# A state-space scan with a routed expert layer on one core: recurrence moved to TensorE and ScalarE, packed score products, one mask operation, six experts loaded before routing ends, and new tables of order

## The chip, the cores and the metric

The kernel runs as one program on one core of a Trainium2 chip. The metric is the device time of that program in microseconds (us), the median of repeated runs. The profile beside it comes from one execution, recorded by the hardware profiler.

## The reference

A chunked state-space scan over `(4 batches, 8 heads, 768 steps, 32 values)` with a state of 16 by 32 per batch and head gives a matrix of 3072 tokens by 256. That matrix goes through a layer of 8 experts: each token goes to the expert with the largest logit, each expert keeps its 80 tokens with the largest gate weight, and all other rows of the output are zero.

```python
cum = np.cumsum(la, axis=-1)                       # la: log of the decay, one chunk
L = np.exp(cum[..., :, None] - cum[..., None, :]) * causal
y_intra = np.einsum('bhij,bhjd->bhid', np.einsum('bhin,bhjn->bhij', Cc, Bc) * L, xc)
y_inter = np.einsum('bhin,bhnd->bhid', Cc, state) * np.exp(cum)[..., None]
state = decay_full[:, :, None, None] * state + np.sum(Bx, axis=2)
...
expert_idx = np.argmax(logits, axis=1)
for e in range(E):
    if len(tok_idx) > capacity:
        tok_idx = tok_idx[np.argpartition(-gw, capacity)[:capacity]]
    h = np.maximum(x[tok_idx] @ w1[e], 0.0)
    out[tok_idx] = gate_w[tok_idx, None] * (h @ w2[e])
```

## The kernel before, in words

**Order of the work.** The scheduling is manual: every engine runs its instructions in the order in which the program's text issues them, and waits only for what an instruction needs. The scan is cut into 12 chunks of 64 steps. The main loop runs over k = 0 to 10; its pass k finishes chunk k and prepares chunk k+1, and k = 11 stands behind the loop by itself. Between the fixed steps the loop calls `slot(plan, i)`, which reads letters from the table `PLAN[k]`: `k` is one step of a routing key, `t` spreads finished keys, `S` and `D` are rank comparisons on ScalarE and VectorE, `s` and `d` shorter ones, `o` and `O` comparisons of a tile with itself on GpSimd and VectorE, `c` the column sums of a comparison on TensorE, `w` a filler product. `LAST` and `REST` order what is left after chunk 11. `WARM` counts filler products at fixed places.

**One chunk.** TensorE multiplies chunk k+1's B by a block-diagonal copy of C (`scores`, tile `cb`): `bd` holds 8 heads side by side with 16 live rows each, so each product contracts all 128 rows to 32 columns, 4 of them 512 wide and 4 half as wide. The first three chunks' blocks are made by 24 scalings on ScalarE and VectorE (`first_blocks`, L683 and L685), the later ones by 8 small transfers per pair of chunks on SP's queue (`spread`, L325), which wait for VectorE's `ct` (`scale_c`, L319). Then come the router's `logits` (tile `rk`), the chunk's sums B times x (`chunk_sums`, tile `vs`, two banks), the part of the output from the state (`inter`), and the part within the chunk (`intra`, tile `yv`). VectorE masks the scores in two operations (`masks`, L346) and adds the carried state to the sums in two (`add_sums`, L368). GpSimd scales x (`scale_x`, L295), writes the state into a block layout by four operations of 32 partitions (`states`, L378, tile `stw`) and the decayed state by one (L384). ScalarE raises the exponents (`widen`, L306), which TensorE turns (`turn`, L312), copies the output (`save_outputs`, L411) and, after TensorE has turned it to token order (`turn_outputs`, L425, tile `mi`), copies it again for the transfer to `y_dram` (`store`, L429).

**Routing.** `keys` (L445 to L509) makes one number per token from the logits, some 22 small VectorE operations per group of 1 or 2 chunks. `turn_keys` lays keys out along the free dimension, and 276 blocks of 128 by 128 comparisons (`take`, L584 and L590) count how many keys of the same expert are larger. `collect` turns ranks into row numbers.

**Experts.** Weights of 4 experts are loaded during the scan (`load_w1`, `load_w2`, L274 and L279, 1 MB each), those of the other 4 into the same buffers as these come free, from SP's queue, one expert's 2 MB per job. `up` and `down` are 64 recorded TensorE products each; rows come by indirect transfers of GpSimd (`gather`, L918) and leave by others (`put_rows`, L976). Filler rows of the output are zeroed by three 1 MB transfers (`clear`, L284).

Line 120 is a helper that issues nearly all products, so profile rows of L120 are told apart by their tiles.

Of the kernel before, what the change touches and what calls it, by code (L numbers as in the profile page):

```python
# [7 lines left out]
F32 = mybir.dt.float32  # L8
# [9 lines left out]
P = 128  # L18
# [13 lines left out]
YT_BUFS = 3  # L32
SP = 4
WARM = (6, 2, 2, 4, 2, 11, 0, 1)
# [3 lines left out]
B0 = (1, 4, 7), ()  # L38
B1 = (0, 1, 4, 7), ()
B2 = (0, 1, 2, 3, 4, 5, 6, 7), ()  # L40
KS = 6
PAIRS = ()
POOLK = ()
POOLS = 15
MOVE = 0
BACK = 1
FAST = 7
PLAN = (
    "||||||",
    "||||||",  # L50
    "||kkk|||kk|sk",
    "||||||",
    "OSSO|c|kkkcc||||",
    "kkkS|||Sc||d|c",
    "||kkkcc||kS|kk|kkk",
    "ckOkkSS||kkkkkkkkc|c||S|kkktk",
    "cOODS|S|kkDccDkkkkkc||S||kkOckk",
    "SSkoct|Ssk|kDkckkkcSk|c|||DS",
    "kStocDSSc|k|kkk|c||dh||",
    "StDckSkkkkkk|cocDcSo|ScS|tkkkhDSckDkkckkoS|Scc|czScc|ccSccccchDkzkcc",  # L60
)
LAST = "ODsiDxiiScSiwDSiicwwiiiwiScwiwSwiDSwciiixcccz"
# [4 lines left out]
C_ID = C_W + 2 * P  # L67
C_H8 = C_ID + P
C_TIE = C_H8 + NH
C_SEL = C_TIE + P  # L70
C_MASK = C_SEL + P
C_WE = C_MASK + 2 * CH
C_BM = C_WE + NE
C_HM = C_BM + 16
C_TH = C_HM + 2
# [9 lines left out]
def const_block():  # L85
# [28 lines left out]
def moe_kernel(ctx: ExitStack, tc: tile.TileContext, cap, tm_d, bn_d, cn_d, aa_d, wg_d, w1_d, w2_d,  # L114
# [15 lines left out]
    cmp_bufs = 5 if cap <= 80 else 3  # L130
# [925 lines left out]
```

## Time and profile before

| what | us |
|---|---|
| median of 3 runs (lowest, highest) | 180.26 (179.71, 183.33) |
| time of the profiled execution | 182.07 |
| its span, first to last instruction | 180.3 |
| start, to the scores of chunk 1 | 0 to 14.66 |
| main loop | 14.66 to 98.55 |
| chunk 11, last keys and comparisons | 98.55 to 117.3 |
| row numbers and first gathers | 117.3 to 125.6 |
| eight experts, last transfer | 125.6 to 180.3 |

In a row of the timeline stand start, duration, engine, line, operation, output and inputs, the number of instructions merged, and in brackets how long the engine had been idle and what ended that. A row of the groups ends with busy time and mean duration of one, then idle time ahead of it. "issue" is idle time for which the trace shows no releaser. A row of the stretches gives the length, then the busy time of PE (TensorE's products), PEld (its weight loads), DVE (VectorE), ACT (ScalarE) and POOL (GpSimd) with instruction counts, the granted TensorE clock, the share of time in which the transfer engines were busy, and what they moved in GB/s. Recorded product durations overlap, so their count times the mean is more than their busy time.

### The profile page before, as it was taken

To read this page: it belongs to the slowest core of one execution; us is meant where nothing else is said; L and a number is where in the kernel's file an instruction comes from. 1 tells how busy PE (TensorE), PEld (TensorE's weight loads), DVE (VectorE), ACT (ScalarE), POOL (GpSimd) and SP (SyncE) were. 2 spreads that over 40 slices of the span, in tenths; PEclk is the share of its full clock that TensorE was granted. 3 is DMA by queue.
4 is the path that set the end of the run, shared out by engine and by line. 5 is a ranking of instruction groups with operands and counts; after the bars stand their busy time and mean duration, and the time that the engine had idled before them with its cause. 6 is when DMAs were issued, how large, how long until landed. Compare 5 with 4: busy or idle time off the path is not lost. (4 is left out here: it accounts for less than half of the span.)

```text
span 180.3 us, 8266 instructions
## 1 busy us (share of the span) xinstructions
PE 144.9 (80%) x3574; PEld 109.2 (61%) x3574; DVE 106.1 (59%) x430; ACT 71.1 (39%) x177; POOL 89.2 (49%) x147
## 2 busy tenths in 40 slices
PE   6578898389859857995998957879988797799980
PEld 2334566276547637583857847734977677689970
DVE  6499549456993999699999999970211011011100
ACT  3795322114225061727677979800212211221120
POOL 8280699363755638149585888907140340422022
PEclk9979999958999997599669955557999999999998
DMA  5981649985993995899653101101399999810000
GB/s 135 344 319 27 215 149 268 317 296 153 343 401 93 293 358 199 230 295 379 219 170 130 62 4 62 58 2 40 105 369 306 291 374 307 297 35 4 22 22 18
DMA packets 22549, 34.75 MB, mean 193 GB/s; under 512 B 2032, under 2 KB 17136, under 8 KB 22512
## 3 DMA queue, kind: packets, MB, share of 16 engines
q1 hardware_dynamic: 21744, 32.91, 54.8%
q0 software_dynamic: 768, 1.31, 2.4%
q8 instruction: 28, 0.46, 1.0%
q14 instruction: 9, 0.07, 0.1%
HBM read 26.08 MB, written 6.95 MB: 183 GB/s over the span
## 5 line engine op out<-in xcount | busy, mean ns | idle before, releaser
L378 POOL TENSOR_TENSOR stw<-rr,alr 32x256 f32<-32x256 f32 x44 | 27.1, 616 | 34.8 <-DVE rr L368 17.4
L976 POOL DMA_INDIRECT out<-og,idx x8 | 7.5, 935 | 37.9 <-DVE og L974 37.9
L120 PE MATMUL yv<-ht,w 128*64 128x80 f32 x512 | 20.8, 235 | 5.6 <-ACT ht L947 5.6
L120 PEld LDWEIGHTS yv<-ht,w 128*64 128x64 f32 x512 | 18.6, 137 | 7.2 <-ACT ht L947 6.4
L120 PE MATMUL cb<-bd,bn 128*32 128x512 f32 (+1 forms) x192 | 20.5, 535 | 2.2 <-ACT ep L306 1.0
L120 PE MATMUL yv<-ct,stw 128*64 128x64 f32 x320 | 17.2, 252 | 6.1 <-issue 5.4
L120 PE MATMUL cb<-xs,w 128*64 128x80 f32 x512 | 20.9, 234 | 0.4 <-DVE xs L931 0.4
L346 DVE TENSOR_TENSOR m<-cb,cst 128x512 f32<-128x512 f32 x24 | 15.4, 684 | 9.2 <-PE cb L120 9.2
L584 ACT ACTIVATE bd<-krow,keb 128x896 bf16<-128x896 f32 (+3 forms) x21 | 20.7, 991 | 0.0
L947 ACT ACTIVATE ht<-cb 128x320 f32<-128x320 f32 x16 | 7.0, 438 | 34.0 <-issue 11.3
L120 PEld LDWEIGHTS cb<-xs,w 128*64 128x64 f32 x512 | 18.9, 137 | 2.0 <-issue 1.3
L120 PEld LDWEIGHTS yv<-ct,stw 128*64 128x64 f32 x320 | 13.5, 157 | 8.2 <-issue 6.4
L974 DVE TENSOR_SCALAR og<-vs,gs 80x256 f32<-80x256 f32 x8 | 3.8, 480 | 24.4 <-PE vs L969 24.4
L429 ACT COPY zs<-mi 128x512 f32<-128x512 f32 x11 | 6.4, 584 | 28.3 <-PE mi L425 27.0
L295 POOL TENSOR_TENSOR xt<-tm,em 128x256 f32<-128x256 f32 x24 | 14.8, 636 | 5.3 <-ACT ep L306 3.5
L931 DVE COPY xs<-mi 128x160 f32<-128x160 f32 x8 | 2.6, 325 | 23.3 <-remote 12.6
L120 PEld LDWEIGHTS cb<-bd,bn 128*32 128x32 f32 x192 | 6.0, 117 | 12.6 <-issue 10.7
L120 PE MATMUL yv<-m,xt 64*32 64x64 f32 x704 | 11.6, 241 | 0.0
L590 DVE TENSOR_SCALAR_CACHE_REDUCE bd<-krow,keb 128x896 bf16<-128x896 f32 (+4 forms) x11 | 11.1, 1018 | 0.3
L918 POOL DMA_INDIRECT xg<-y_dram,idx x8 | 7.9, 991 | 6.6 <-issue 6.6
L120 PE MATMUL vs<-xt,tm 64*32 64x64 f32 x352 | 6.2, 231 | 5.5 <-issue 5.5
L120 PEld LDWEIGHTS yv<-m,xt 64*32 64x32 f32 x704 | 7.7, 117 | 3.5 <-issue 2.7
(153 smaller groups left out, 285.6 us busy)
## 6 DMA issues: line engine op xcount, KB each, us to landing
w<-w SPq DMA_DIRECT2D x16, 1024.0 KB, 7.5
tm<-tm SPq DMA_DIRECT2D x5, 768.0 KB, 6.0
y_dram<-zs SPq DMA_DIRECT2D x12, 256.0 KB, 2.6
out<-zrow SPq DMA_DIRECT2D x3, 1024.0 KB
cn<-cn SPq DMA_DIRECT2D x6, 256.0 KB, 6.1
bn<-bn SPq DMA_DIRECT2D x6, 256.0 KB, 3.9
bd<-ct SPq DMA_DIRECT2D x32, 32.0 KB, 5.5
tm<-tm SPq DMA_DIRECT2D x2, 384.0 KB, 5.9
```

The lines of the kernel that those rows point to most:

```text
L120: T.matmul(out=o, lhsT=l, rhs=r, start=start, stop=stop, skip_group_check=True, **kw)
L295: G.tensor_tensor(out=xt[:, p].rearrange("p (h d) -> p h d", h=NH), in0=tm[:, p].rearrange("p (h d) -> p h d", h=NH), in1=em[:, p, c, :, N ...
L346: V.tensor_tensor(out=m, in0=cb[p].rearrange("p (h i) -> p h i", h=NH), in1=cst[:, None, C_MASK + p * CH:C_MASK + (p + 1) * CH].broadcast_ ...
L378: G.tensor_tensor(out=stw[(c + 1) % 2][q, hp].rearrange("p b (r d) -> p (b r) d", r=2), in0=rr[q].rearrange("p b (r d) -> p (b r) d", r=2) ...
L429: S.copy(out=zs.rearrange("p t d -> p (t d)"), in_=z)
L584: S.activation(out=cmpt[:, 0:n], in_=rows, func=AF.Sign, scale=2.0 ** -24 - 1.0, bias=keb[:, t:t + 1], accum_out=acs[:, t, col:col + 1])
L590: V.tensor_scalar(out=cmpt[:, 0:n], in0=rows, scalar1=keb[:, t:t + 1], scalar2=None, op0=ALU.is_le, op1=ALU.add, accum_out=acc[:, t, col:c ...
L918: G.indirect_dma_start(out=xg[n % NX][0:cw], out_offset=None, in_=y_dram[:, :], in_offset=bass.IndirectOffsetOnAxis(ap=idx[0:cw, s, e:e + ...
L931: V.tensor_copy(out=xs, in_=mi[:, 0:2 * P].rearrange("p (k t) -> p k t", k=2)[:, :, 0:cw])
L947: S.activation(out=ht[:, f - 3:f + 1], in_=cb[f // 4].rearrange("p (f t) -> p f t", f=4)[:, :, 0:cw], func=AF.Relu)
L974: V.tensor_scalar(out=og[0:cw], in0=vs[n % 2][0:cw, 0:D], scalar1=gs[0:cw, s, e:e + 1], scalar2=None, op0=ALU.mult)
L976: G.indirect_dma_start(out=out, out_offset=bass.IndirectOffsetOnAxis(ap=idx[0:cw, s, e:e + 1], axis=0), in_=og[0:cw], in_offset=None, boun ...
```

## The change

Heads and batches are laid out in another order, so that a pair of heads fills 32 partitions. `bd` then needs 2 blocks per chunk in place of 8, and is made from `ct` by one ScalarE and one VectorE operation for every chunk; `spread`, `first_blocks` and their transfers are gone. `scores` becomes 16 products of 32 rows by 64 columns, 128 wide. The exponents go through 8 products of 64 by 64. The state has no block layout: TensorE adds it to the chunk's sums by a product with the identity, ScalarE copies the sum, GpSimd scales it in one operation. The two masks become one operation of 1024. The logits become 8 further columns of the product that turns the output. `vs` is one bank, `cb`, `yv` and `mi` are pairs of banks. GpSimd memsets of `bd` and `stw` at the start are gone, the first clip of `a` is split in two, constants come in three transfers by order of use. Weights come in parts of 512 KB with rows laid out contiguously by the host: six experts before routing ends, the last two during jobs 1 to 4. Some loads wait for a one-element write ("token") of VectorE, ScalarE or GpSimd into their target. `out` is cleared in 12 pieces. `BACK` goes from 1 to 5, and the tables are new.

```diff
-WARM = (6, 2, 2, 4, 2, 11, 0, 1)
+WARM = (8, 3, 5, 4, 2, 8, 0, 2)
...
-    "kStocDSSc|k|kkk|c||dh||",
+    "SSSSt|c|Sllwskckwkz|hwDS|D|OokDSoOocO|Scckll|",
...
+    def load_ahead(n):
+        i = order.index(jobs[n][0])
+        if slow and order.index(slow[0][0]) < i + W_EARLY + W_LATE:
+            load_slow(hold)
...
+    def scale_c(c, u, act):
+        cts[c] = ct = work.tile([P, 256], F32, name="ct", bufs=5)
+        V.tensor_tensor(out=ct, in0=cns[c], in1=u, op=ALU.mult)
+        for r in range(2):
+            o, m = bd[c % 3][:, r], cst[:, C_HM + r:C_HM + r + 1]
+            if r < act:
+                S.activation(out=o, in_=ct, func=AF.Copy, scale=m)
+            else:
+                V.tensor_scalar(out=o, in0=ct, scalar1=m, scalar2=None, op0=ALU.mult)
...
+    def scores(c):
+        for b in range(NB):
+            for g in range(2):
+                for q in range(2):
+                    r = slice(g * CH + 32 * q, g * CH + 32 * q + 32)
+                    mm(cb[q][g * CH:(g + 1) * CH, b * P:(b + 1) * P].rearrange("p (r i) -> p r i", r=2),
+                       bn[r, b * CH:(b + 1) * CH], bdc[r, :, b * CH:(b + 1) * CH], b == 0, True,
+                       tile_position=(r.start, g * CH))
...
     def masks(c):
+        m = work.tile([P, 2 * NH, CH], F32, name="m")
+        V.tensor_tensor(out=m, in0=cb2.rearrange("p q (h i) -> p (q h) i", h=NH),
+                        in1=cst[:, None, C_MASK:C_MASK + CH].broadcast_to([P, 2 * NH, CH]), op=ALU.mult)
...
     def chunk_sums(c):
+        if c:
+
+            mm(vs[:, 0:256], ident, stw[c % 2], False, True)
...
     def add_sums(c):
+        rr = work.tile([P, 256], F32, name="rr")
+        S.copy(out=rr, in_=vs[:, 0:256])
...
     def states(c):
-        for hp in range(4):
-            q = slice(32 * hp, 32 * hp + 32)
-            G.tensor_tensor(out=stw[(c + 1) % 2][q, hp].rearrange("p b (r d) -> p (b r) d", r=2),
...
+        G.tensor_tensor(out=stw[(c + 1) % 2].rearrange("p (b d) -> p b d", d=HD),
...
     def turn_outputs(c, z):
+                mm(z[:, p, g * P:(g + 1) * P + NE], yts[c][:, p, g], wi[:, g], g == 0, True)
```

**TensorE in one chunk.** Before, chunk 2, from the end of its scores to the first half of the second state product (`vs` and `yv` are pairs of banks, told apart by their numbers; `rk<-wg,yt` are the logits, `vs<-cst,ep` the turned exponents):

```order
L120 MATMUL cb_82<-bd_118,bn 32x8x32
L120 MATMUL rk<-wg,yt 32x8 x16
L120 MATMUL vs_85<-xt,tm 32x64 x8
L120 MATMUL vs_86<-xt,tm 32x64 x8
L120 MATMUL yv_83<-ct,stw_119 64x64 x4
L120 MATMUL yv_84<-ct,stw_119 64x64 x4
L120 MATMUL yv_83<-m,xt 32x64 x8
L120 MATMUL yv_84<-m,xt 32x64 x8
L312 MATMUL vs_85<-cst,ep 128x128 x2
L312 MATMUL vs_86<-cst,ep 128x128 x2
L120 MATMUL yv_83<-ct,stw_119 64x64 x4
```

And a whole chunk of the change, chunk 1 (`vs<-stw,cst` is the state added by the identity, `mi<-wi,yt` the turned output with the logits, `rk<-zer,ones` a filler):

```order
L118 MATMUL cb<-bd_121,bc 64x128 x16
L118 MATMUL vs<-xt,tm 32x64 x16
L118 MATMUL vs<-stw_123,cst 128x256
L118 MATMUL mi<-wi,yt 128x136 x4
L118 MATMUL yv<-ct,stw_123 64x64 x16
L118 MATMUL yv<-m,xt 32x64 x16
L118 MATMUL vs<-cst,ep 64x64 x8
L118 LDWEIGHTS ones
L118 MATMUL rk<-zer,ones 128x192
L118 MATMUL yv<-m,xt 32x64 x16
```

The logits are gone as a step, the turned output has moved from behind the state products to ahead of them, the state products stand in one piece, and one product with the identity is new.

**GpSimd in two chunks.** Before, from x of chunk 3 on:

```order
L295 TENSOR_TENSOR xt<-tm,em 128x256 x2
L378 TENSOR_TENSOR stw_119<-rr,alr 32x256 x4
L384 TENSOR_TENSOR st<-rr,alp 128x256
L295 TENSOR_TENSOR xt<-tm,em 128x256 x2
L378 TENSOR_TENSOR stw_120<-rr,alr 32x256 x4
```

The same place in the change:

```order
L348 TENSOR_TENSOR xt<-tm,em 128x256 x2
L404 TENSOR_TENSOR stw_122<-rr,alr 128x256
L326 MEMSET tm 1x1
L326 MEMSET zrow 1x1
L348 TENSOR_TENSOR xt<-tm,em 128x256 x2
```

Five operations on the state became one, with two one-element tokens behind it.

**SP's queue around the experts.** Before, the last stores of the scan and the first loads of the experts stage:

```order
L430 DMA y_dram<-zs 128x2x256 x3
L274 DMA w_2683<-w 128x2x1024
L279 DMA w_2685<-w 128x8x256
L274 DMA w_2771<-w 128x2x1024
L279 DMA w_2773<-w 128x8x256
```

In the change (rows of 1024 values are the 512 KB parts):

```order
L311 DMA out<-zrow 256x1x256 x2
L303 DMA w_2233<-w 128x1024 x2
L303 DMA w_2323<-w 128x1024 x2
L447 DMA y_dram<-zs 128x512
L303 DMA w_2762<-w 128x1024 x2
L303 DMA w_2852<-w 128x1024 x2
L303 DMA w_2942<-w 128x1024 x2
L303 DMA w_3032<-w 128x1024 x2
```

The fifth and sixth expert's loads now stand ahead of the last store, and eight parts are left for the experts stage where there were eight transfers of twice the size.

More of the change, by code (lines that the diff above doesn't have):

```diff
@@ new lines, in moe_kernel @@
+    pp = pairs.enter_context(tc.tile_pool(name="pp", bufs=1, space=PSUM))
+    cb2, yv2, tz = [pp.tile([P, 2, 512], F32, name=n) for n in ("cb", "yv", "mi")]
+    cb, yv, mi = [cb2[:, i] for i in range(2)], [yv2[:, i] for i in range(2)], tz[:, 0]
+    vs = ps.tile([P, 512], F32, name="vs")
+    rk = ps.tile([P, 512], F32, name="rk")
+    R0 = NT * NE
+    cst = const.tile([P, NC_CONST], F32, name="cst")
+    n = NT * NH
+    aa = const.tile([P, n + 3 * CH], F32, name="aa")
+    wi = const.tile([P, 2, P + NE], F32, name="wi")
@@ L573, in take @@
             cq.pop(0)
[L574 to L580 removed]
+        while len(sums) >= CMP_BUFS:
+            column_sums(1)
+        cmpt = cmpp.tile([P, PB, P], BF16, name="cmp")
         rows = krow[:, i0:i0 + n]
@@ L710, in moe_kernel @@
     V.memset(gt[:, :, 0:1], 1.0)
-    G.memset(stw[0], 0.0)
     G.memset(zrow, 0.0)
@@ L782, in moe_kernel @@
     plan = PLAN[k]
-    give(1)
-    inter(k, 0)
-    logits(k - 1)
+    inter(k)
+    turn_outputs(k - 1, tz)
+    unsaved.append((k - 1, tz))
     start_keys(k - 1, 1)
@@ L793, in moe_kernel @@
     save_outputs(k)
+    phase.close()
+    work = ctx.enter_context(tc.tile_pool(name="ffn", bufs=2))
+    late_pool = ctx.enter_context(tc.tile_pool(name="late", bufs=1))
+    wpool2.append(ctx.enter_context(tc.tile_pool(name="wpool2", bufs=W_LATE)))
+    for i in range(NCH - 2, NCH):
+        clear(i)
+    pt = late_pool.tile([P, NT // 2, P, 2], BF16, name="pt")
+    if cap < P:
+        G.memset(pt[:, :, cap:].rearrange("p u w v -> p u (w v)").bitcast(F32), 0.0)
     slot(plan, 2)
-    logits(k)
+    turn_outputs(k, yv2)
+    unsaved.append((k, yv2))
     start_keys(k, 1)
     turns.append(k)
-    turn_outputs(k - 1, mi)
-    unsaved.append((k - 1, mi))
     slot(plan, 3)
-    turn_outputs(k, yv[0])
-    unsaved.append((k, yv[0]))
     slot(plan, 4)
@@ L846, in moe_kernel @@
         pass
-    for i in range(2):
-        G.memset(stw[i].rearrange("p a b c -> p (a b c)")[:, 0:NT // 4 * P], 0.0)
     i = 0
@@ L858, in moe_kernel @@
     own_sums()
-    busy(WARM[4])
-    phase.close()
-    work = ctx.enter_context(tc.tile_pool(name="ffn", bufs=2))
-    late_pool = ctx.enter_context(tc.tile_pool(name="late", bufs=1))
+    busy(WARM[4], mi)
+    pairs.close()
+    pb = ctx.enter_context(tc.tile_pool(name="pb", bufs=1, space=PSUM))
+    banks = [pb.tile([P, 512], F32, name=f"bk{i}") for i in range(6)]
+    cb, yv, mi, lo = banks[0:2], banks[2:4], banks[4], banks[5]
     NX = 4
```

596 lines of the change are left out of this document (272 added, 324 removed).

## The prediction

> **What bounds the kernel now.** I read the stretches of the span first, since an average over the whole hides that its stages have different limits, then the loop chunk by chunk, then one chunk's timeline of PE, and the waits and groups last. The stretches, with the columns PE, PEld, DVE, ACT, POOL, granted clock, DMA share and GB/s behind the length:
>
> ```profile
> 0.00:14.66 14.66, 9.23 (x72) 4.03 (x73) 10.27 (x24) 10.45 (x25) 8.61 (x12) 0.88 0.74 247
> 14.66:98.55 83.89, 69.78 (x2025) 50.02 (x2025) 67.59 (x282) 34.02 (x87) 48.40 (x79) 0.88 0.74 243
> 98.55:117.30 18.75, 14.60 (x396) 12.75 (x387) 17.97 (x91) 16.06 (x36) 16.61 (x41) 0.64 0.14 45
> 117.30:125.60 8.30, 6.86 (x46) 2.75 (x43) 3.40 (x16) 0.00 (x0) 3.19 (x4) 0.59 0.07 21
> 125.60:176.50 50.90, 44.41 (x1054) 39.62 (x1054) 6.90 (x20) 10.63 (x32) 11.46 (x14) 1.00 0.57 189
> ```
>
> The loop is nearly half of the span. In it PE is busy for 69.78 of 83.89 us, DVE for 67.59 and the transfers for 0.74 of the time, so three limits lie close together: what PE gives up can be had back only down to DVE's work. In the tail (98.55 to 117.30) DVE sets the pace with 17.97 of 18.75. In the experts stage PE does. The loop by chunks, same columns:
>
> ```profile
> 24.70:31.03 6.33, 5.77 (x185) 3.98 (x186) 4.60 (x19) 1.16 (x4) 5.88 (x10) 1.00 0.67 195
> 31.03:42.43 11.40, 7.99 (x188) 6.06 (x189) 6.97 (x31) 2.26 (x7) 6.20 (x11) 0.70 0.76 254
> 63.17:74.44 11.27, 8.21 (x206) 6.47 (x206) 10.96 (x62) 4.79 (x12) 5.65 (x10) 0.78 0.75 255
> ```
>
> An undisturbed chunk takes 6.3 us, of which PE is busy for 5.77. Two chunks with nearly the same number of products take over 11, at a granted clock of 0.70 and 0.78. PE's waits in the loop, as total, times and longest:
>
> ```profile
> PE vs L120 <- issue: 5.5, 2, 3.4
> PE yv L120 <- issue: 5.4, 3, 3.1
> ```
>
> So 10.9 us of PE's idle 14.1 (83.89 less 69.78) have no releaser that the trace shows. The chunk of 6.33, PE alone:
>
> ```profile
> 24.70 1.62 PE L120 MATMUL cb<-bd,bn 128*32 128x512 f32 x16
> 26.11 0.50 PE L120 MATMUL rk<-wg,yt 128*32 128x8 f32 x32
> 26.54 0.48 PE L120 MATMUL vs<-xt,tm 64*32 64x64 f32 x32
> 26.95 0.69 PE L120 MATMUL yv<-ct,stw 128*64 128x64 f32 x16
> 27.56 0.48 PE L120 MATMUL yv<-m,xt 64*32 64x64 f32 x32
> 27.98 0.66 PE L312 MATMUL vs<-cst,ep 128*128 128x128 f32 x4
> 28.56 0.34 PE L120 MATMUL yv<-ct,stw 128*64 128x64 f32 x4
> 29.39 0.57 PE L120 MATMUL yv<-ct,stw 128*64 128x64 f32 x12 [0.49 <-issue]
> 29.89 0.66 PE L425 MATMUL mi<-cst,yt 128*128 128x128 f32 x4
> 30.48 0.48 PE L120 MATMUL yv<-m,xt 64*32 64x64 f32 x32
> ```
>
> **The change, stage by stage. Start.** The rows up to the scores of chunk 1:
>
> ```profile
> 1.63 3.51 POOL L193 MEMSET bd<- 128x4096 f32 x1
> 3.19 2.16 DVE L209 TENSOR_SCALAR aa<-aa 128x384 f32<-128x384 f32 x1 [0.73 <-DMA aa<-aa]
> 5.39 0.36 ACT L210 ACTIVATE la<-aa 128x192 f32<-128x192 f32 x1 [3.15 <-DVE aa L209]
> 6.02 1.28 ACT L306 ACT_TABLE_LOAD   x1
> 7.78 0.99 PE L312 MATMUL vs<-cst,ep 128*128 128x128 f32 x4 [0.86 <-ACT ep L306]
> 9.15 3.01 DVE L685 TENSOR_SCALAR bd<-ct,cst 128x256 f32<-128x256 f32 x5
> 13.82 1.29 DVE L346 TENSOR_TENSOR m<-cb,cst 128x512 f32<-128x512 f32 x2
> 14.66 2.00 PE L120 MATMUL cb<-bd,bn 128*32 128x512 f32 x16 [0.89 <-DVE m L346]
> ```
>
> The clip of `a` (L209) takes 2.16 and ends with the memset of `bd` beside it, at about 5.2; two logarithms of 0.36, the table load of 1.28 and the exponents follow. The memset goes and the clip is halved. For the half clip I take 0.36, as the logarithm of 192 values: 3.19 + 0.36 + 0.36 + 0.35 + 1.28 + 0.36 for the exponents + 0.50 for half of the 0.99 gives 6.4 for the first turned exponents. Of 24 scalings (5 of them in the quoted 3.01) 6 are left, three on each engine: VectorE then has three `ct` of 0.41, three scalings of 0.52 and two copies of 0.35, together 3.5, which ends at 9.9. Scores 0 are done by then, and the mask of 1.2 lets scores 1 start at 11.1 in place of 14.66. I take **−3.5**. If transfers of the constants come later than that, −2; if the work on VectorE is hidden beside the exponents, −4.5.
>
> **Loop.** The rows that bear on VectorE, GpSimd and ScalarE (a row of the groups ends with busy, mean ns | idle before and releasers):
>
> ```profile
> L378 POOL TENSOR_TENSOR stw<-rr,alr 32x256 f32<-32x256 f32 x44 | 27.1, 616 | 34.8 <-DVE rr L368 17.4 <-DVE mx L445 8.2 <-DVE alr L246 6.7
> L346 DVE TENSOR_TENSOR m<-cb,cst 128x512 f32<-128x512 f32 x24 | 15.4, 684 | 9.2 <-PE cb L120 9.2
> L368 DVE TENSOR_TENSOR rr<-vs,st 128x128 f32<-128x128 f32 x20 | 4.9, 280 | 4.7 <-PE vs L120 3.0 <-POOL st L384 1.7
> L685 DVE TENSOR_SCALAR bd<-ct,cst 128x256 f32<-128x256 f32 x9 | 4.1, 521 | 0.0
> L319 DVE TENSOR_TENSOR ct<-cn,vs 128x256 f32<-128x256 f32 x10 | 3.8, 412 | 1.5 <-PE vs L312 1.4
> L411 ACT COPY yt<-yv 128x256 f32<-128x256 f32 x22 | 7.1, 378 | 0.0
> ```
>
> PE's chunk before, in steps that follow each other at 24.70, 26.11, 26.54 and so on: scores 1.5, logits 0.5, sums 0.48, state products 0.69 twice, within the chunk 0.48 twice, exponents and turned output 0.66 each. Less what overlaps that is about 5.8. Of the change I price:
>
> - scores: 16 products of 32 rows by 64 columns, 128 wide. Each uses half of the columns and a quarter of the rows, so four can run side by side. Upper bound the 1.5 of before; lower bound 0.48, the row of 32 recorded products 64 wide. At double that width I take 0.96;
> - sums 0.48 as before. The state's identity product is 256 wide: the four turnings in 0.66 are 512 columns together, so 0.35;
> - turned output with the logits' 8 columns 0.70 (0.66 times 136/128); state products as 16 of 64 by 64, with half the rows and so two side by side, from 0.48 to 0.69, taken 0.55; within the chunk 0.96 as before; exponents in 8 products of a quarter of the array 0.30 (0.17 if four are side by side, 0.66 if none).
>
> Together 4.30: 1.5 less per chunk, 16.5 less in 11. Some 22 more filler products stand in the loop's fixed places, 0.2 each, +4.5. PE's work is then 57.8, and with its idle 14.1 left as it is the loop takes 71.9.
>
> VectorE is the next limit. Its mask becomes one operation of 1024, 1.23 in place of twice 0.684; two additions of 0.280 go to TensorE and ScalarE (a copy of 0.378 there, which ScalarE hides: 34.0 busy of 83.9); against that it gets one scaling of 0.521 in each chunk. The logits' operations, keys that move to GpSimd, tokens and comparisons add up to about −0.5; in all VectorE goes from 67.6 to some 65.5. GpSimd gives up four operations of 616 ns for one as wide, so its 48.4 falls to some 30, and the chain from sums to the next chunk's state products is shorter: copy 0.38 and one scaling of 0.62 stand where one addition of 0.28 and four scalings of 616 stood. What would be late next is the mask, which waits 9.2 for scores in the row above, and scores get shorter too. VectorE so near to the loop costs some more waiting: I take +1, and 73 for the loop, **−11**. The bounds are 64 (VectorE's work nearly without a gap) and 84 (no gain, because PE's idle grows by as much as its work falls).
>
> SP's queue loses 64 transfers of 32 KB for `bd`, which the trace shows holding the queue while they wait for `ct`; so loads start earlier. The loop moved 243 GB/s over 83.89 us, 20.4 MB. With five or six experts' weights, less `bd` and with the clears I count 20.5 to 21 after. At 243/0.74 = 328 GB/s with all engines busy that takes 64 us: it fits in 73, at a share near 0.88.
>
> **Tail and row numbers.** VectorE's comparisons there fall from 5,888 to 4,992 values per partition; ScalarE has as many as before, 16.06 of busy time: **−1**, with 0 as the one end (ScalarE decides) and −2 as the other. Three fewer fillers in the row numbers: **−0.5** (0 to −1.2). The last transfer is as before.
>
> **Experts.** TensorE's `down` products where each job starts:
>
> ```profile
> 142.81 1.88 PE L120 MATMUL yv<-ht,w 128*64 128x80 f32 x48 [1.29 <-ACT ht L947]
> 149.72 1.88 PE L120 MATMUL yv<-ht,w 128*64 128x80 f32 x48 [1.33 <-ACT ht L947]
> 161.45 2.62 PE L120 MATMUL yv<-ht,w 128*64 128x80 f32 x64
> 167.01 2.57 PE L120 MATMUL yv<-ht,w 128*64 128x80 f32 x64
> ```
>
> A job takes 6.91 us (142.81 to 149.72) while 2 MB are loaded beside it, and 5.56 (161.45 to 167.01) when none are. Four jobs are of the first kind. The change loads 1 MB in each of the same four. Without any hold-up the gain is 4 × 1.35 = 5.4; with the same hold-up as before nothing. The half of the bytes came up late by the queue's place before, and now stand as 512 KB parts with long rows, so I take three quarters, **−4**.
>
> **The sum**: −3.5 −11 −1 −0.5 −4 = −20, on a span of 180.3: 160.3. The profiled execution took 182.07, 1.77 over its span, and the median of the runs shown is 180.26, 1.81 under that execution. So an execution like the profiled one would take 162.1, and the median **160.3**.
>
> **The rivals.**
>
> *Transfers or PE's unexplained stalls hold the loop* (0.20). For it: PE's 10.9 us of "issue" fall into chunks in which much is moved (254 GB/s against 195 in the quick one), and the change wants the same bytes in less time. Against it: the share of the loop is 0.74, and the eight small transfers are gone. The loop stays at 84 and the rest gives −8 to −9: **172**.
>
> *The stalls go* (0.12). For it: the two chunks of 11.3 lose 5 us each against the one of 6.33, at a lower granted clock; if loads no longer collide there, 10 more come off, to the bound of 64 for VectorE: **150**. Against it: nothing in the diff touches what PE waits for there.
>
> *Row groups of TensorE take turns* (0.06, the slower side). Before, products of 64 rows of one kind go to pairs of banks (`vs_85` and `vs_86`, `yv_83` and `yv_84`, one bank per row group); in the change two or four row groups write one bank, at different partitions. If such products cannot run side by side, each is priced like the turnings: 0.165 for 128 columns, 0.083 for 64. Then a chunk takes 2.64 (scores) + 1.33 (sums) + 1.33 (state) + 0.66 (exponents) + 0.35 + 0.70 + 0.96 = 7.97 in place of 4.30, 40 us more in 11 chunks: **200**. It decides from 4.30 + 20/11 = 6.1 us per chunk on. For it, in the trace of before: no group of 64-row products goes to one bank. Against it: nothing there shows such a case waiting. The Trainium skill, "TensorEngine Tiling (Array Packing)", section "Restrictions and Gotchas", states that different row tiles cannot access the same PSUM bank simultaneously; that speaks against this change, and no run here shows it so far. By that rule the time is the one of this rival, and without it that of the sum.
>
> *Nothing gained* (0.04): loads collide with the start, and waits for tokens on SP's queue let inputs come late: **180**.
>
> **How the numbers follow.** The forecast has 0.58, the four rivals 0.20, 0.12, 0.06 and 0.04. The forecast's own range is 154 to 166. To hold 8 of 10 I take in the stalls that go and most of the case in which transfers hold the loop: **148 to 174**. Faster by over 2%, which is about what a measurement of this kernel can tell from no change, are the forecast and the first two rivals less a rest: 0.86; within 2% 0.06; slower 0.08.
>
> **What would show it.** Right: scores 1 at about 11; a chunk without a stall in 5 to 5.5 us with PE at 4.3 plus fillers; VectorE at over 85% of the loop; job periods of 5.6 to 5.9 us throughout; a tail of about 17.5. Wrong: PE's products of `cb` or `vs` lasting 2.6 or 1.3 per chunk (row groups take turns); "issue" waits of PE that grow beyond 11 (the stalls move with the loads); a loop of 64 with no such waits; mask or `ct` late because ScalarE's copy of the state queues behind its comparisons.

## The result and the profile after

The change takes 165.86 us (median of 4 runs, 165.03 to 166.67) where the kernel before takes 180.59 us (median of 4, 179.71 to 183.33, with the runs beside it). The ratio is 0.920 (95% interval 0.913 to 0.927): faster by 14.7 us, where 20 were forecast. The profiled execution took 166.67 us with a span of 164.9. In the experiments further down, runs of one kernel differed by up to 7.4 us, so stages of the profiled executions are compared there: kernels with the same text in the loop took 73.2 to 75.8 us for it, the change, `after_again` and `ends`, alike in the tail, 22.6 to 23.9 there, and differences inside these bounds are not read.

The stretches of the changed kernel, cut at the same events as before: scores of chunk 1, state products of chunk 11, fillers ahead of the row numbers, first `up`. Columns as in the table of the prediction.

```profile
0.00:11.52 11.52, 9.53 (x133) 5.98 (x134) 5.74 (x21) 6.18 (x12) 1.44 (x6) 1.00 0.76 249
11.52:85.42 73.90, 66.60 (x2088) 54.08 (x2088) 51.51 (x252) 36.97 (x90) 33.93 (x84) 0.98 0.79 252
85.42:108.47 23.05, 17.83 (x334) 15.90 (x332) 20.34 (x116) 18.19 (x42) 12.43 (x38) 0.56 0.81 279
108.47:115.30 6.83, 4.83 (x36) 2.13 (x35) 2.12 (x8) 0.00 (x0) 3.11 (x3) 0.74 0.09 24
115.30:161.10 45.80, 44.81 (x1054) 40.81 (x1054) 6.89 (x20) 11.23 (x40) 12.95 (x21) 0.96 0.39 118
```

| stage | before | after | difference | forecast |
|---|---|---|---|---|
| start | 14.66 | 11.52 | -3.1 | -3.5 |
| loop | 83.89 | 73.90 | -10.0 | -11 |
| chunk 11, last keys, comparisons | 18.75 | 23.05 | +4.3 | -1 |
| row numbers | 8.30 | 6.83 | -1.5 | -0.5 |
| experts with the last transfer | 54.70 | 49.60 | -5.1 | -4 |
| span | 180.3 | 164.9 | -15.4 | -20 |

Four stages came near their term, and the tail went the other way. The loop's size is right, but the columns contradict its working: PE is busy for 66.6 us where 57.8 were forecast, VectorE for 51.5 where 65.5 were, and PE's idle time, which was to stay at 14.1, is 7.3. PE's waits there, by the view of waits:

```profile
PE vs L118 <- issue: 1.6, 2, 1.1
PE yv L118 <- issue: 1.5, 3, 0.7
PE cb L118 <- issue: 0.5, 1, 0.5
```

The waits without a releaser are 3.6 us in place of 10.9, and the clock of the loop is 0.98 in place of 0.88. One chunk without a stall, PE alone:

```profile
15.22 1.10 PE L118 MATMUL cb<-bd,bc 32*64 32x128 f32 x32
16.26 0.65 PE L118 MATMUL vs<-xt,tm 64*32 64x64 f32 x32
16.84 0.70 PE L118 MATMUL vs<-stw,cst 128*128 128x256 f32 x2
17.37 1.09 PE L118 MATMUL mi<-wi,yt 128*128 128x136 f32 x8
18.39 0.69 PE L118 MATMUL yv<-ct,stw 32*64 32x64 f32 x32
19.02 0.45 PE L118 MATMUL yv<-m,xt 64*32 64x64 f32 x32
19.40 0.68 PE L118 MATMUL vs<-cst,ep 64*64 64x64 f32 x16
```

From start to start: scores 1.04, sums 0.58, identity 0.53, turned output with logits 1.02, state 0.63, exponents 0.62, and twice 0.38 within the chunk make 5.2 us, where 4.30 were forecast and the chunk before took about 5.7 by its rows. The products became only 0.5 us shorter per chunk.

In the tail (chunk 11, last keys, comparisons) both engines that compare have more to do. Before, then after, by the groups of the stage:

```profile
L584 ACT ACTIVATE bd<-krow,keb 128x896 bf16<-128x896 f32 (+3 forms) x13 | 12.7, 984 | 0.0
L590 DVE TENSOR_SCALAR_CACHE_REDUCE bd<-krow,keb 128x896 bf16<-128x896 f32 (+2 forms) x8 | 8.2, 1040 | 0.2
```

```profile
L589 ACT ACTIVATE cmp<-krow,keb 128x512 bf16<-128x512 f32 (+3 forms) x17 | 15.7, 928 | 0.2 <-DVE w L329 0.2
L595 DVE TENSOR_SCALAR_CACHE_REDUCE cmp<-krow,keb 128x896 bf16<-128x896 f32 (+4 forms) x10 | 8.9, 927 | 0.6 <-PE rk L118 0.5
L552 DVE SCALAR_TENSOR_TENSOR tj<-cst,key,krow 128x128 bf16<-128x128 f32 x4 | 2.5, 662 | 1.0 <-ACT krow L535 1.0
```

ScalarE makes 17 comparisons there in place of 13, VectorE 10 in place of 8, and 4 of a tile with itself that GpSimd made before. In the experts stage all jobs start 5.4 us apart, with loads beside them or not:

```profile
119.59 2.43 PE L118 MATMUL bk<-ht,w 128*64 128x80 f32 x64
124.95 2.43 PE L118 MATMUL bk<-ht,w 128*64 128x80 f32 x64
```

### The profile page after: what moved, and what is told of

It is laid out like the page before. It is cut to its first block, busy times and chain, and to the rows that moved or that the text cites. A ratio compares the mean times of both kernels' runs of the same rounds, so it can differ in the third digit from the quotient of the medians.

```text
span 164.9 us, 8428 instructions
## 1 busy us (share of the span) xinstructions
PE 143.6 (87%) x3639; PEld 118.9 (72%) x3640; DVE 86.6 (53%) x415; ACT 72.6 (44%) x182; POOL 64.7 (39%) x152
## 4 chain that ended last, share of the span: by engine, by line
PE 70%; ACT 9%; DVE 8%; issue 7%; DMA 4%; POOLq 1%; POOL 0%; ACTq 0%
PE bk L118 24%; PE vs L118 11%; PE mi L118 9%; PE yv L118 9%; PE rk L118 7%; PE cb L118 6%; ACT cmp L589 4%; PE vs L533 2%; DMA bc<-bc 2%; DVE cmp L595 2%; ACT zs L445 2%; PE bk L924 1%; DMA out<-og,idx 1%; ACT krow L535 1%; DVE m L378 1%
## 5 line engine op out<-in xcount | busy, mean ns | idle before, releaser
L589 ACT ACTIVATE cmp<-krow,keb 128x512 bf16<-128x512 f32 (+6 forms) x32 | 28.1, 884 | 0.2 <-DVE w L329 0.2
L118 PE MATMUL bk<-xs,w 128*64 128x80 f32 x512 | 22.5, 245 | 0.5 <-DVE xs L930 0.4
L118 PEld LDWEIGHTS bk<-xs,w 128*64 128x64 f32 x512 | 20.4, 146 | 2.2 <-issue 1.6
L118 PE MATMUL bk<-ht,w 128*64 128x80 f32 x512 | 19.6, 234 | 0.0
L118 PEld LDWEIGHTS bk<-ht,w 128*64 128x64 f32 x512 | 18.3, 137 | 0.8
L595 DVE TENSOR_SCALAR_CACHE_REDUCE cmp<-krow,keb 128x512 bf16<-128x512 f32 (+6 forms) x21 | 16.9, 828 | 0.7 <-PE rk L118 0.5
L118 PE MATMUL mi<-wi,yt 128*128 128x136 f32 x88 | 13.6, 298 | 2.9 <-ACT yt L429 2.4
L118 PE MATMUL rk<-zer,ones 128*128 128x192 bf16 (+1 forms) x61 | 13.6, 302 | 1.4 <-DVE halfs L202 1.4
L378 DVE TENSOR_TENSOR m<-cb,cst 128x1024 f32<-128x1024 f32 x12 | 14.6, 1216 | 0.0
L118 PE MATMUL cb<-bd,bc 32*64 32x128 f32 x384 | 13.9, 282 | 0.5 <-issue 0.5
L118 PEld LDWEIGHTS <-cmp 128*128 128x128 bf16 x276 | 11.4, 104 | 2.4 <-DVE cmp L595 1.2
L118 PEld LDWEIGHTS cb<-bd,bc 32*64 32x64 f32 x384 | 10.9, 136 | 1.6 <-issue 0.9
L969 ACT COPY ot<-bk 128x80 f32<-128x80 f32 x16 | 3.6, 226 | 15.4 <-PE bk L118 15.4
```

Of the source, the lines that this page charges most:

```text
L118: T.matmul(out=o, lhsT=l, rhs=r, start=start, stop=stop, skip_group_check=True, **kw)
L378: V.tensor_tensor(out=m, in0=cb2.rearrange("p q (h i) -> p (q h) i", h=NH), in1=cst[:, None, C_MASK:C_MASK + CH].broadcast_to([P, 2 * NH, ...
L589: S.activation(out=cmpt[:, 0:n], in_=rows, func=AF.Sign, scale=2.0 ** -24 - 1.0, bias=keb[:, t:t + 1], accum_out=acs[:, t, col:col + 1])
L595: V.tensor_scalar(out=cmpt[:, 0:n], in0=rows, scalar1=keb[:, t:t + 1], scalar2=None, op0=ALU.is_le, op1=ALU.add, accum_out=acc[:, t, col:c ...
L969: S.copy(out=ot[:, k], in_=z[:, 0:cw])
```

## The experiments

The cuts are those of the table above. "Stalls" are PE's waits without a releaser in the loop; all times in us.

| kernel | median | ratio to before (95%) | start | loop | stalls | tail | clock in the tail |
|---|---|---|---|---|---|---|---|
| the change | 165.86 | 0.920 (0.913 to 0.927) | 11.5 | 73.9 | 3.6 | 23.1 | 0.56 |
| `after_again` | 170.24 | 0.916 (0.897 to 0.935) | 10.8 | 75.5 | 3.3 | 23.9 | 0.57 |
| `no_holds` | 171.91 | 0.940 (0.911 to 0.968) | 10.9 | 78.0 | 7.8 | 22.5 | 0.75 |
| `pool_back` | 170.40 | 0.925 (0.914 to 0.935) | 11.0 | 77.0 | 3.6 | 21.8 | 0.72 |
| `logits_first` | 171.17 | 0.921 (0.905 to 0.938) | 10.8 | 75.1 | 3.6 | 23.1 | 0.60 |
| `no_tail_loads` | 170.68 | – | 10.9 | 72.3 | 1.7 | 23.3 | 0.58 |
| `keys_first` | 164.64 | 0.919 (0.908 to 0.930) | 10.9 | 77.4 | 4.1 | 22.5 | 0.75 |
| `warm_tail` | 167.08 | 0.927 (0.914 to 0.940) | 11.4 | 73.2 | 3.6 | 24.8 | 0.70 |
| `best` | 169.57 | – | 11.0 | 75.2 | 4.5 | 24.8 | 0.80 |
| `ends` | 166.12 | 0.920 (0.901 to 0.939) | 11.6 | 75.8 | 4.6 | 22.6 | 0.76 |

The kernel before took 185.54, 185.66 and 182.08 in the three sets.

**What do the products cost, and does sharing a bank matter?** `m_tiles` sets groups like these behind the last job (eleven in all, of which two are shown):

```diff
+    for i in range(64):
+        g, q, r, rr = rc(i)
+        T.matmul(**tile_mm(A[0][rr, 0:64], r, slice(0, 32), 64, (g * CH, rr.start)))
...
+    for i in range(16):
+        T.transpose(out=A[i // 2 % 2][:, 0:128], in_=cst[:, 0:128], identity=ident)
```

> Behind the last job of the changed kernel stand nine groups of products that compute nothing of the result, each cut off from the next by four copies of VectorE: 64 products in the shape of the sums into one bank and into two, 64 in the shape of the scores with two and with four banks, 32 in the shape of the exponents with one and with two banks, 64 in the shape of the state products with two and with four banks, then 16 products of 128 by 136, 16 transposes of 128 by 128 and 8 products by the identity, 256 wide. Theory A (row groups that share a bank hinder each other): the form with more banks is faster in each pair, the sums by a third (18 against 13 ns a recorded product, as the two profiles have them), the scores likewise. Theory B (the price is in the shape, banks do not matter): both forms of a pair agree within 5%. For the turned output both expect that a product of 128 by 136 shows two recorded products and costs near twice a transpose, about 0.25 against 0.15 us.

There are eleven groups where the expectation says nine. The timeline of PE, at a granted clock of 1.00 throughout. L1042 and L1047 are the sums with one and two banks, L1052 and L1057 the scores with two and four, L1062 and L1067 the exponents with one and two, L1072 and L1077 the state products with two and four, then the product of 136, the transpose and the identity:

```profile
167.99 1.99 PE L1042 MATMUL bk<-cst 64*32 64x64 f32 x128
170.39 2.30 PE L1047 MATMUL bk<-cst 64*32 64x64 f32 x128 [0.41 <-DVE bin L1044]
173.01 4.11 PE L1052 MATMUL bk<-cst 32*64 32x128 f32 x128 [0.31 <-DVE bin L1049]
178.22 4.03 PE L1057 MATMUL bk<-cst 32*64 32x128 f32 x126 [0.29 <-DVE bin L1054]
182.43 2.08 PE L1062 MATMUL bk<-cst 64*64 64x64 f32 x64 [0.18 <-DVE bin L1059]
184.91 2.40 PE L1067 MATMUL bk<-cst 64*64 64x64 f32 x64 [0.39 <-DVE bin L1064]
187.59 2.48 PE L1072 MATMUL bk<-cst 32*64 32x64 f32 x128 [0.28 <-DVE bin L1069]
191.10 2.40 PE L1077 MATMUL bk<-cst 32*64 32x64 f32 x126 [0.40 <-DVE bin L1074]
193.78 3.97 PE L1081 MATMUL bk<-cst 128*128 128x136 f32 x32 [0.28 <-DVE bin L1079]
197.68 2.21 PE L1085 MATMUL bk<-cst 128*128 128x128 f32 x16
200.06 3.72 PE L1089 MATMUL bk<-cst 128*128 128x256 f32 x16 [0.17 <-DVE bin L1087]
```

More banks are in no pair faster by more than 2% per recorded product: 1.99 against 2.30, 4.11 against 4.03 (for two fewer), 2.08 against 2.40, 2.48 against 2.40 (for two fewer). So theory A falls, and with it the rival in which row groups take turns on a bank. Theory B's 5% holds for the scores and the state products alone; in the other two pairs the form with more banks is 15% slower, which stays open. The Trainium skill, "TensorEngine Tiling (Array Packing)", section "Restrictions and Gotchas", says that different row tiles cannot access one PSUM bank simultaneously; where they write different partitions of it, as here, the runs show no cost. What costs is the shape, per recorded product 16 ns (64 by 32, 64 wide), 19 (32 by 64), 33 (64 by 64) and 32 (32 by 64, 128 wide). A product of 128 by 136 is recorded twice and takes 0.25 us (3.97 over 16), a transpose once and 0.14 (2.21 over 16).

**What were PE's stalls?** Theory A takes them for waits for the next block of PE's own instructions. `before_few_loads` thins the loads of the kernel before:

```diff
-    slow = [lambda e=e, f=f: f(e, nc.sync) for e in order[:4] for f in (load_w1, load_w2)]
+    slow = [lambda f=f: f(order[0], nc.sync) for f in (load_w1, load_w2)]
+    slow += [lambda e=e, i=i: wt.__setitem__(e, wt[order[0]]) for e in order[1:4] for i in range(2)]
```

> The kernel before, with the loads of three of the four experts left out of the loop (their jobs use the weights of the first, so the routed result is another); 6 MB of 20.4 are missing there. Theory A (fetches of instructions queue behind data): PE's waits without a releaser fall from 10.9 to under 4 us and the loop from 83.9 to 72 to 77, at a granted clock over 0.95 in place of 0.88. Theory B (the stalls have to do with the program's text or products): they stay at 9 to 11 and the loop over 82.

Its loop, as stretch and as waits of PE:

```profile
15.32:97.20 81.88, 65.88 (x2025) 47.61 (x2026) 67.96 (x286) 34.25 (x87) 48.59 (x80) 0.96 0.55 173
```

```profile
PE rk L120 <- DVE dl L450: 6.0, 6, 1.8
PE vs L120 <- issue: 3.7, 1, 3.7
PE yv L120 <- issue: 2.3, 3, 1.1
```

With 0.5 for `cb` the stalls fall from 10.9 to 6.5 and the clock rises from 0.88 to 0.96, between what the two theories gave; by this one profile loads have to do with them. But the loop only falls from 83.9 to 81.9, since VectorE, busy for 68 of 82 us, now holds PE up (6.0 in place of 2.3 for `dl`), and the whole kernel takes 188.16, no less than the kernel before in its set. This run splits the loop of before: at a clock of 0.96 the old products keep PE busy for 65.9 us, the new ones for 66.6 at 0.98.

`no_holds` takes the one-element writes out of the change's loop and tail:

```diff
-                load_slow(pause)
+                load_slow()
...
-            load(k + 3, token)
+            load(k + 3)
...
-            token(zrow[0:1, 0:1])
```

> The changed kernel without the one-element writes that hold back loads and clears in the main loop; nothing else differs. Theory A (the stalls of PE without a releaser are waits for a block of its own instructions, which queue behind data when loads come in bursts, and the change removed them by holding loads back): loads bunch again, PE's waits of that kind in the loop grow from 3.6 to 8 us or more, the loop from 73.9 to over 79, the kernel by 3 to 6%. Theory B (the small transfers of the block-diagonal C caused them): nothing changes, within 1%.

Waits of PE in its loop, and the loop:

```profile
PE yv L118 <- issue: 3.2, 3, 1.2
PE cb L118 <- issue: 2.6, 2, 2.1
PE vs L118 <- issue: 2.0, 2, 1.3
```

```profile
10.94:88.98 78.04, 66.65 (x2087) 54.12 (x2088) 49.51 (x236) 36.91 (x89) 33.18 (x66) 0.98 0.72 237
```

The stalls are 7.8, against 3.3 to 4.6 in the five profiles with the same loop otherwise; PE's busy time does not move, and the loop is 2.2 to 4.8 us longer than theirs. That is theory A just short of its numbers (8 and 79). The whole kernel's interval is too wide to show it.

What is late at a stall can be read beside it. The view of transfers counts the queue of instructions, whose packets are 16 KB each. In the kernel before, in the quarter of a microsecond from 34.25:

```profile
q8 instruction: 1, 0.02, 25.4%
```

and PE afterwards:

```profile
36.64 0.42 PE L120 MATMUL vs<-xt,tm 64*32 64x64 f32 x3 [3.42 <-issue]
```

| kernel | record of the packet starts | stall ends |
|---|---|---|
| before | 34.30, 50.79, 66.01, 83.33 | 36.64, 53.16, 68.55, 85.54 |
| `no_holds` | 16.42, 21.25, 27.00, 36.38, 59.73, 66.55 | 18.90, 23.56, 29.21, 38.61, 62.00, 68.85 |

These ten stalls, all without a releaser that last over 0.7 us in the two loops, end 2.2 to 2.5 us after such a packet. They also stand at fixed distances in PE's own instructions. The stretches between the ends of the four stalls of before:

```profile
36.64:53.16 16.52, 13.94 (x381) 10.38 (x382) 13.60 (x59) 4.95 (x15) 9.46 (x16) 0.83 0.85 288
53.16:68.55 15.39, 11.47 (x381) 8.57 (x381) 12.06 (x56) 5.89 (x15) 8.15 (x14) 1.00 0.80 268
68.55:85.54 16.99, 14.64 (x381) 10.69 (x382) 14.75 (x69) 8.42 (x20) 10.18 (x17) 0.80 0.84 267
```

Products and weight loads together are 763, 762 and 763; with PE's 5 or 6 waits for semaphores, which the columns leave out, each stretch has 768 instructions within one, three times 256. In `no_holds` the same sums are 254, 256, 506, 1275 and 255: near one, one, two, five and one times 256. In the loop of before there are 16 packets, and PE's 2025 products and 2025 weight loads make 15.8 blocks of 256. So the stalls are waits of PE for its next block of instructions. Why a block comes late is less firm: in the 3 us ahead of the packet the transfer engines were busy for 0.93 to 1.06 of the time at the four stalls of before and for 0.62 to 0.98 at the six of `no_holds`, but they were as full ahead of others that held nothing up (1.00 ahead of the one at 54.80). No run changed the fetches themselves. The Trainium skill, "Runtime: NRT & Kernel Launch", section "Instruction fetch mechanics", describes blocks of 256 instructions fetched by a queue of their own and calls the cost mostly hidden; the block agrees with the packets and the distances here, the cost does not, with 3.4 us at a time.

**Was it the small transfers?** `small_back` puts transfers of `ct` back, to tiles that nothing reads:

```diff
...
             scale_c(k + 3, vs[:, 256:], ACTB)
+            if k % 2:
+                for h in range(NH):
+                    r = slice(h * NST, (h + 1) * NST)
+                    for i in range(2):
+                        nc.sync.dma_start(out=bx[k // 2 % 2][r, i, 0:256], in_=cts[k + 2 + i][r])
```

> The changed kernel with the small transfers of before put back beside the rest: per pair of chunks ct is sent in 16 transfers of 16 KB into tiles that nothing reads, at the place in SP's queue where the block-diagonal copy was made. Theory A (it is bursts of large loads): SP's queue waits for ct again and loads behind it bunch, so PE's waits without a releaser grow from 3.6 to some 6 to 10 us and the loop to 77 to 82. Theory B (it is only the number of small packets): much the same growth, but with loads still spread out, DMA share under 0.85 at the stalls. If neither holds: loop within 1 us of 73.9.

```profile
PE cb L118 <- DMA bc<-bc: 20.1, 4, 7.4
PE vs L118 <- issue: 2.7, 2, 1.4
```

193.85 us, slower than the kernel before in its set, with a loop of 100.3. Neither theory foresaw it: the stalls stay at 3.0, but PE waits four times, 20.1 us in all, for an input (`bc`) that stands in SP's queue behind the 16 transfers. These hardly wait for `ct` (SP's queue does so for 1.7 us in the loop); to issue one takes the queue 0.59 us on the median, up to 1.9, so that the first 16 fill it from 19.2 to 33.0, and the `bc` for which PE waits until 39.8 is issued at 34.95. Small transfers do not make stalls; the time to issue them costs inputs. The kernel before issues 40 such transfers at 0.58 us on the median, loads inputs for two chunks at a time, and shows no such wait.

**Why did VectorE's work fall so far?** Of the 16 us some 12 are in the small operations of the keys. `pool_back` brings GpSimd's busy time in the loop near to that of before (45.8 us, before 48.4, the change 33.9):

```diff
...
+        for i in range(2):
+            G.tensor_tensor(out=idle, in0=rrs[c], in1=rrs[c], op=ALU.mult)
```

> The changed kernel with two operations of 128 by 256 on GpSimd put behind each state operation, writing a tile that nothing reads, so that GpSimd is as busy in the loop as before (48 us in place of 34). Theory A (VectorE's small operations got shorter because GpSimd works less beside them): the q operations grow from 176 ns towards the 300 of before, VectorE's busy time in the loop from 51.5 to 55 to 60. Theory B (they are shorter because they are other operations): their means stay within 10%, VectorE's busy time within 1 us. Loop under both 74 to 78, more under A.

One key operation in the loop of the kernel before, of the change and of `pool_back`:

```profile
L475 DVE SCALAR_TENSOR_TENSOR q<-fr 128x32 f32<-128x32 f32 (+1 forms) x18 | 5.2, 339 | 0.0
```

```profile
L490 DVE SCALAR_TENSOR_TENSOR q<-fr 128x16 f32<-128x16 f32 (+1 forms) x16 | 2.1, 182 | 0.0
```

```profile
L493 DVE SCALAR_TENSOR_TENSOR q<-fr 128x16 f32<-128x16 f32 (+1 forms) x16 | 3.3, 254 | 0.0
```

At 16 elements this operation takes 309, 178 and 260 ns, so it goes more than half of the way back; other key operations move both ways, and VectorE's busy time is 52.3 against 51.5 (51.2 in `after_again`): A's first number and B's second. GpSimd's busy time, brought back in this form, accounts for about 1 of the 16 us; where the rest of the 12 comes from stays open.

**Why is the tail longer?** Five kernels, beside a control, `after_again`, the change unaltered:

> The changed kernel as it is, once more, so that the others of this set can be compared with it on the same chip. All theories: loop 73 to 75 us, PE's waits without a releaser in the loop near 3.6, from chunk 11's state products to the fillers ahead of the row numbers 23 us; 0.91 to 0.93 of the kernel before.

Its loop and tail (75.5 and 23.9) are 1.6 and 0.9 longer than those of the first profile; the ratio agrees.

`logits_first` takes chunk 10's and 11's logits out of the turned output:

```diff
+                mm(z[:, p, P:P + NE], yts[c][:, p, g], wi[:, g, (1 - g) * P:(1 - g) * P + NE], g == 0, g == 1)
...
+                T.transpose(out=z[:, p, g * (P + NE):g * (P + NE) + P], in_=yts[c][:, p, g], identity=ident)
...
-    turn_outputs(k, yv2)
+    turn_late(k, yv2)
```

> For chunks 10 and 11 alone the logits are products of 8 columns ahead of the turned output, and this is made by transposes as before; nothing is left out. Theory A (the tail is longer because the last logits wait in a product of 136 columns that costs two passes): chunk 11's logits come 1.5 us sooner after its output copy, the tail falls from 23 to about 21, the kernel by 1 to 1.5%. Theory B (VectorE and ScalarE are full in the tail): the tail stays within 0.5 us.

Tail 23.1: theory B. `no_tail_loads` leaves two experts' loads out:

```diff
+                if order.index(e) in (4, 5):
+                    wt[e] = wt[order[order.index(e) - 2]]
+                    continue
```

> The loads of the fifth and sixth expert are left out, their jobs use the weights of the third and fourth (so their part of the result is another); 4 MB fewer, mostly in the tail. Theory A (the loads in the tail cost something there, as transfers of outputs, fetches of instructions or tokens wait): the tail falls from 23 to under 21.5 us. Theory B (they are free there, the tail being VectorE's and ScalarE's work): it stays within 0.5 us. The jobs of the experts stage stay at 5.4 to 5.7 us each under both.

The transfers' share of the tail falls from 0.81 to 0.29, the tail stays at 23.3: the loads are free there. Its expectation on jobs failed: those with loads beside them took 6.2 to 6.6 us, as in every profile of the changed kernels in the first two sets, while in the change's own profile and in the last set, on another chip, all took 5.4 to 5.7. In `after_again` PE stalls for 1.7 us in these jobs without a releaser; before, ScalarE's `ht` was waited for.

`keys_first` and `warm_tail`:

```diff
-    "SSSSt|c|Sllwskckwkz|hwDS|D|OokDSoOocO|Scckll|",
+    "SSSSt|c|Sllwskckwkz|hwDS|D|kkkkkkkkOokDSoOocO|Scckll|",
```

```diff
     inter(k)
+    busy(11)
     turn_outputs(k - 1, tz)
```

> In pass 10 the remaining steps of chunk 9's keys are put ahead of two comparisons of a tile with itself and one of a longer row on VectorE; nothing is added or left out. Theory A (the tail is longer because chunk 9's keys are ready 5.0 us after the loop in place of 1.7, and all later steps follow them): they are ready some 2.5 us sooner and the tail falls from 23 to 21 to 21.5. Theory B (VectorE's and ScalarE's work fills the tail whatever the order): the keys are sooner, the tail stays within 0.5 us.

> Eleven filler products stand where TensorE waits 2.1 us for chunk 10's output copy behind ScalarE's comparisons. Theory A (that wait lowers the granted clock, and the tail's products at half speed make it longer): the clock of the tail rises from 0.56 to over 0.65 and the tail falls by 1 to 1.5 us. Theory B (the clock follows the tail's many short waits, not this one, or nothing in the tail waits for TensorE): clock under 0.62 or a tail within 0.5 us of 23.

With the keys first, the tail is 22.5, no clear difference (theory B): chunk 9's keys are ready 4.4 us after the loop in place of 5.8, and not the 2.5 sooner that were expected. With fillers the clock rises to 0.70, and the tail is longer (24.8), which neither theory gave. Its waits of PE say why:

```profile
PE rk L118 <- issue: 4.0, 1, 4.0
PE vs L533 <- DVE q L513: 2.7, 2, 2.5
```

The wait of 2.1 us for the output copy has gone, and a stall of 4.0 stands in its place, which ends 2.4 us after a packet of instructions. In the change's own profile a stall of 0.5 stands three products behind the wait for the copy: PE had been waiting for two things at once, and the fillers took away the one that showed.

`best` joins both, and moves the comparisons of a tile with itself in `PLAN[10]`, `PLAN[11]` and `LAST` to GpSimd:

```diff
-    "SSSSt|c|Sllwskckwkz|hwDS|D|OokDSoOocO|Scckll|",
+    "SSSSt|c|Sllwskckwkz|hwDS|D|kkkkkkkkookDSooococ|Scckll|",
...
+    busy(11)
```

> Keys of chunk 9 first, the fillers, and all comparisons of a tile with itself in the last two tables on GpSimd in place of VectorE (2.6 us of VectorE's work in the tail). Theory A (order, clock and VectorE's work each cost something): the tail falls from 23 to 19.5 to 21 us, the kernel by 1 to 2% against the change. Theory B (GpSimd or ScalarE then holds the tail): within 1 us of 23.

It isn't better: tail 24.8, with a stall of 3.9 at the same edge of a block, and 169.57 us, which neither theory gave. VectorE has lost its four comparisons of a tile with itself (2.5 us), but its busy time there only falls from 20.3 to 20.0, as some of the key operations last longer. So logits, loads, key order and these comparisons are each out as the main cause, and the clock is not sufficient.

The traces show where the time goes. ScalarE's copies of the last two outputs (`yt`, of chunk 10, then of chunk 11), before, then after, and the wait of PE for the first of them after:

```profile
98.73 0.66 ACT L411 COPY yt<-yv 128x256 f32<-128x256 f32 x2
102.99 0.63 ACT L411 COPY yt<-cb 128x256 f32<-128x256 f32 x2
```

```profile
87.60 0.57 ACT L429 COPY yt<-yv 128x512 f32<-128x512 f32 x1
93.55 0.59 ACT L429 COPY yt<-cb 128x512 f32<-128x512 f32 x1
```

```profile
PE mi L118 <- ACT yt L429: 2.1, 1, 2.1
```

| us after the end of the loop | before | the change |
|---|---|---|
| chunk 10's output copied | 0.8 | 2.7 |
| chunk 11's output copied | 5.1 | 8.7 |
| last keys ready | 13.2 | 16.4 |
| last comparison done | 17.9 | 22.3 |
| end of the stage | 18.75 | 23.05 |

Chunk 10's copy ends 1.9 us later than before: it stands behind comparisons that ScalarE still has from the loop. Chunk 11's ends 3.7 us later; the other 1.7 lie between the two copies and are not assigned. From there on the stage takes 14.3 us in place of 13.7. In `warm_tail` and `best`, with the longest tails, it ends 11.1 and 11.0 us after the loop. So most of the 4.3 us is a late start of the last chunk's routing, and little is work behind it. This is read from the traces: no run moved the copies.

**Start and experts.** `ends`:

```diff
-BACK = 5
+BACK = 1
...
+    for i in range(5):
+        G.memset(free, 0.0)
```

> Two stages far apart are altered: at the start GpSimd writes 4140 values per partition of zeros to a tile that is not needed yet, as long as the memset of before; in the experts stage the turning back of a job's rows stands where it stood before the change (BACK 1). Theory A (the memset held up the first clip, and the half loads, not the place of the turning, brought the jobs to 5.4 us): scores of chunk 1 start 1.5 to 3 us later than the 10.8 to 11.5 of the change, the jobs take 5.4 to 5.8 us. Theory B (the clip is long by itself; the wait for the turning back made jobs long): scores of chunk 1 within 0.5 us, the jobs 6 us or more.

The scores of chunk 1 start at 11.64, within 0.5 of the change's 11.52 (theory B), though the clip's two halves take 1.10 with the zeroing beside them in place of 0.43: the second half is longer, and the exponents wait for the first alone. Five pieces of 0.86 are not one of 3.51, so what that one held up is not shown. The jobs stay at 5.4 to 5.6 with `BACK` 1 (theory A): the place of the turning is worth nothing there. Which of the smaller loads, their rows and their place in the queue made the jobs shorter, no run separates.

## Why the forecast came out as it did

**The start** (-3.5, measured -3.1). The first turned exponents started at 6.47, forecast for 6.4. By the rows the half clip (0.43 for both halves) and the few scalings carry it, though no run takes them back; that the memset mattered by itself is not shown.

**The loop** (-11, measured -10.0) is right in size by luck: its working is wrong. PE's busy time came out 8.8 us longer than worked out and its idle time 6.8 shorter, and VectorE had far less to do than counted:

- "Together 4.30" should have been 5.2. The largest misses are the turned output, 1.02 for 0.70, and the exponents, 0.62 for 0.30. Both were priced like transposes, which are recorded once, while the change makes them ordinary products, which are recorded twice: the x4 of the old row and the doubled counts of the other products were both at hand. The identity was 0.53 for 0.35 for the same reason. The shorter products, forecast to give 16.5 us, give 0.5 times 11, about 5.5, which the 25 fillers in the loop (5.1) and other products take back: PE's busy time, 65.9 at nearly full clock before (in `before_few_loads`), is 66.6 after.
- "Its idle 14.1 left as it is" failed: it fell to 7.3, with the stalls from 10.9 to 3.6 and the clock from 0.88 to 0.98. This was the rival to which 0.12 was given, and its argument against ("nothing in the diff touches what PE waits for") was wrong. The diff spreads loads out in time by one-element writes and smaller parts; `no_holds` shows that the writes are worth 3 to 4.5 of the 7 us. The rest is not assigned.
- "Some 65.5" for VectorE was 51.5. `before_few_loads` had PE's busy time of the change and some of its stalls gone, and stayed at 82 with VectorE at 68: fewer stalls alone were not enough. What less VectorE work gives alone, no run shows.

**Transfers holding the loop** did not come: it took 73.9 us at a share of 0.79, with 18.6 MB where 20.5 to 21 were counted. The prediction reads 64 transfers of 32 KB for `bd` out of the trace, which hold SP's queue while they wait for `ct`; the profile has 32 of 32 KB and 8 of 16 KB, and the queue waits 3.7 us in all for `ct` there.

**Row groups taking turns** was wrong, and is settled: in `m_tiles` more banks are not faster.

**The tail** is the step that failed: -1 forecast, +4.3 measured. It missed by 5.3 us, the other four stages together by 0.7 the other way, and the sum by 4.6. "VectorE's comparisons there fall from 5,888 to 4,992 values" and "ScalarE has as many as before" were counted at a place in the program; the engines run behind the program, and work issued in the loop is done after it. In the profile, added up by the forms of the groups above, VectorE's comparisons in this stage rise from 6,400 to 6,912 values per partition and ScalarE's from 10,752 to 13,056. VectorE is busy for 2.4 us longer, and idle for 2.7 us in place of 0.8. The term also had work alone and no path to the last keys, and most of the 4.3 us lies there: chunk 11's output copy ends 3.7 us later. The prediction's last sign of being wrong, a copy of ScalarE that queues behind its comparisons, came for the output and not for the state.

**Row numbers and experts** (-4.5, measured -6.6). The jobs with loads run at 5.4 us, no longer than others, so the full 5.4 was to be had and three quarters of it was too careful; in the profiles of the first two sets the same jobs take 6.2 to 6.6, so this term can come out at 1 us per job less.

## What to carry to other kernels

Count whether a product is recorded once or twice before pricing it by another: a transpose's row is no price for a product of the same size. A wait without a releaser that recurs on the busiest engine is worth a look at the instruction queue and at how loads are bunched before it is written down as fixed. Work of engines that run behind the program is counted in the trace's time, not at the program's line. A stage's end is priced by the path to its last input too, and a wait is not removed by filling it when a second one lies under it.

## What the runs showed of the hardware

- PE stalled for up to 4.0 us without a releaser. In two loops all such stalls of over 0.7 us stood 256 of its instructions or a multiple apart and ended 2.2 to 2.5 us after a 16 KB packet on the instruction queue. Without the writes that hold loads back they came to 7.8 us per loop, against 3.3 to 4.6.
- After the stalls of 3.42, 3.06 and 2.04 us in the loop of before the granted clock fell, after that of 1.83 it did not (1.00 from 53.16 to 68.55): from the end of the first to the chunk's end it was 0.52, and 16 state products took 1.12 us in place of 0.69.
- Products of different row groups into one PSUM bank, at different partitions, cost no more than into several banks (1.99 against 2.30 us for 128).
- To issue a small transfer took SP's queue 0.59 us on the median (64 of 16 KB in `small_back`).
- A recorded product of 32 rows by 64 columns, 128 wide, took 32 ns, one of 64 wide 19 ns, and one of 64 rows by 32 columns, 64 wide, 16 ns; each of these uses an eighth of the array, and one of 64 by 64, a quarter, took 33 ns at 64 wide.
